# Chunk 6 of an attention and Swish kernel: six pairs of h by half-size products, and the numerators ahead of two groups of h

## The chip, the core and the metric

The kernel runs on one core of one Trainium2 chip. The metric is the device time of one execution in microseconds (us), lower is better. The median of 7 runs of the kernel before is 281.01 us (280.42 to 281.57).

A core has engines that run side by side, each taking its own list of instructions in order: TensorE (PE in the profile; PEld are its weight loads) multiplies matrices into PSUM, an accumulator memory of 8 banks; VectorE (DVE) and ScalarE (ACT) do elementwise work and move results out of PSUM; GpSimd (POOL) and SyncE (SP) mostly issue DMA transfers here. An instruction waits on semaphores for the data and the buffers that it needs, and everything behind it on the same engine's list waits with it.

## The reference

Two stages, one after the other. The first is linear attention with cosine weights over 8 batches, 8 heads, 576 positions and 64 channels:

```
phi(x) = concat(relu(x) * cos(theta), relu(x) * sin(theta))      theta = pi/2 * position / 576
kv  = sum over positions of phi(k)^T v;   z = sum over positions of phi(k)
out = (phi(q) kv) / (phi(q) z + 1e-6)
```

The second takes the result as x, 4608 tokens of 512 features (tokens run over batches and positions), through two matrices with a Swish between them:

```
h = x @ w_in                     # 512 -> 2048
g = h * sigmoid(beta * h)
result = g @ w_out               # 2048 -> 512
```

## The kernel before

**Chunks and batches.** The second stage runs in nine chunks c = 0 to 8 of 512 tokens. For a chunk, h is made in 16 groups of 128 features ("jt" 0 to 15), each 128 features x 512 tokens in one PSUM bank; ScalarE applies Silu with a scale of beta and writes g to SBUF (the factor 1/beta is folded into w_out). Then the output products make the result. While chunk c is worked on, the attention of batch b = c + 1 is done in between: K (the products k^T v on TensorE, L272), kt (kv copied out of PSUM by VectorE, L284), N (the numerators q kv, L293, 144 small matmuls in three parts of 48, each into two neighbouring banks), and x0, x1, x2 (per part: denominators L304, reciprocal L308, multiply L315 on VectorE, and transposing DMAs on SP, L363, that write the next chunks' x). In chunk 6 this is the last batch, b = 7; chunks 7 and 8 have no attention.

**Two ways to make h.** A plain group (`h_plain`, L428; "p0" to "p7" in the order, with its Silu "sp0" to "sp7") is 4 matmuls of 512 columns. A pair of groups can instead be made by `h_fast` (L474): a Winograd form of Strassen's scheme with 7 products instead of 8, each of 2 matmuls of 256 columns, on sums of the weights (made in chunk 4) and on sums t1 to t4 of the chunk's x (VectorE, L873, made for the next chunk during the output products). A pair has three banks (b, e, a) and these operations: products 1, 5, 6, 2, 7, 3, 4 on TensorE; c1 and cu, copies of bank b by ScalarE (L499, L501); c5, a copy of bank e by VectorE (L500); a2, a3, a7, additions by VectorE (L502, L504, L503) that complete the two groups in banks a and b; Sa and Sb, their Silus (L419). So product 3 adds to bank e after c5 has read it, a3 needs product 3 and cu, Sa needs a2 and a3, and Sb needs a7 and product 4. Until Sa and Sb have read the banks, nothing else may write them.

The output products are made in the same way (`o_fast`, L552): two halves x and y of seven products each, of 8 matmuls, on the g of even or odd groups and on sums S1 to S4 of g, which VectorE makes group by group (L399; "s34" is S4 for the last quarter of the groups).

**What sets the order.** Nothing is scheduled by a planner: the order in which the program issues instructions is the order on each engine's list. From chunk 5 on it is written out by hand: `chunk` (L894) walks a string of short names, `ORDER` (L852) for chunks 5 and 6 and `ORDER_END` (L859) for 7 and 8, and issues each name's instructions. "X1" is product 1 of pair X, "c1X" its copy c1, "SaX" its Silu; "ox1" and "oy1" are output products, "c1o" and "c1y" their copies, "o2x" their additions; "s01" is S1 for the first quarter of the groups; "K", "kt", "N0" and "x0" as above; "t1" is a sum of the next chunk's x. Names of one engine keep their order in the string, and names of different engines are tied by data and banks alone.

In `ORDER` four pairs are fast: X (groups 0, 1), Y (4, 5), Z (8, 9), V (12, 13), and eight groups are plain; in `ORDER_END` six are fast, with E (2, 3) and F (6, 7), and four plain. The tables `steady` and `end` in `chunk` give each pair its first group and its banks b, e, a; `plain_bank` gives the plain groups theirs; `parts` (L985) are the first banks of the three parts of N, and `xb`, `yb` (L986) the banks of the output products.

In chunk 6 before, the string's end runs "... V4 s21 s23 s14 SbV s22 N0 sp7 ox1 ...": the numerators come after all 16 groups.

Of the kernel before, what the change touches and what calls it, by code (L numbers as in the profile page):

```python
# [22 lines left out]
def kernel(  # L23
# [16 lines left out]
    B, H, S, D = q.shape  # L40
# [10 lines left out]
    E = D + 1  # L51
# [211 lines left out]
    def kv_out(jp, bank):  # L263
        return ps[:, bank : bank + 2, jp * 2 * E : (jp + 1) * 2 * E]

    def kv_mm(b, jp, bank, jjs=(0, 1)):
        t = kv_out(jp, bank)
        for n in range(NQ):
            for jj in jjs:
                for g in range(2):  # L270
                    hs = slice(g * HP, (g + 1) * HP)
                    nc.tensor.matmul(  # L272
                        t[jj * HP : (jj + 1) * HP, g], lhsT=rk[hs, n, 2 * jp + jj, :],
                        rhs=vb[hs, n, 2 * jp + jj].rearrange("q s e -> q (s e)"),
                        start=(n == 0), stop=(n == NQ - 1))
# [189 lines left out]
    def h_fast(c, jt0, banks):  # L465

        b_bank, e_bank, a_bank = banks
        hf = TCH // 2
        b_ps, e_ps, a_ps = (ps[:, k, 0:hf] for k in banks)
        xt, n = xt_tile(c), NB // 2  # L470

        def prod(dst, left, right, start, stop):
            for g in range(2):
                nc.tensor.matmul(dst, lhsT=left[:, g], rhs=right[:, :, g * HP : (g + 1) * HP], start=start and g == 0,  # L474
                                 stop=stop and g == 1, skip_group_check=True)

        def w(f, jp):
            f += jt0 % 4
            return win[jt0 // 4][:, 2 * jp : 2 * jp + 2, f * P : (f + 1) * P]

        def x(jp, i):
            return xt[:, i * n : (i + 1) * n, jp]

        s1, s2, s3, s4 = (w_sum(jt0, i) for i in range(4))
        t1, t2, t3, t4 = (wx["x"][:, i] for i in range(4))
        p1 = part.tile([P, HM], FP32, name="p1", tag="p1")
        p5 = part.tile([P, HM], FP32, name="p5", tag="p5")
        u = part.tile([P, HM], FP32, name="u", tag="u")

        acc = dict(op=ALU.add)  # L490
        ops = {
            "1": lambda: prod(b_ps, w(0, 0), x(0, 0), True, False),
            "5": lambda: prod(e_ps, s1, t1, True, False),
            "6": lambda: prod(b_ps, s2, t2, False, False),
            "2": lambda: prod(a_ps, w(0, 1), x(1, 0), True, True),
            "7": lambda: prod(b_ps, s3, t3, False, False),
            "3": lambda: prod(e_ps, s4, x(1, 1), False, True),
            "4": lambda: prod(b_ps, w(1, 1), t4, False, True),
            "c1": lambda: nc.scalar.copy(p1, b_ps),  # L499
            "c5": lambda: nc.vector.tensor_copy(p5, e_ps),  # L500
            "cu": lambda: nc.scalar.copy(u, b_ps),  # L501
            "a2": lambda: nc.vector.tensor_tensor(a_ps, a_ps, p1, **acc),  # L502
            "a7": lambda: nc.vector.tensor_tensor(ps[:, b_bank, hf:TCH], b_ps, p5, **acc),  # L503
            "a3": lambda: nc.vector.tensor_tensor(ps[:, a_bank, hf:TCH], e_ps, u, **acc),  # L504
            "Sa": lambda: h_silu(c, jt0, a_bank),
            "Sb": lambda: h_silu(c, jt0 + 1, b_bank),
        }
        return ops
# [336 lines left out]
    def k_piece(b, j):  # L845
# [10 lines left out]
        "sp6 s13 SaV V4 s21 s23 s14 SbV s22 N0 sp7 ox1 s31 ox5 s32 k1 x0 c1o s33 ox6 k0 k2 k3 c5o oy1 "  # L856
        "s24 ox2 s34 g0 g1 v8 w4 v4 x1 c1y o2x ox3 v2 v7 cuo x2 oy6 ox7 oy2 cuy o3x o7x oy5 oy7 ox4 w8 "
        "o2y v6 c5y t1 t3 oy3 w1 w0 o7y t2 v5 v3 oy4 t4 o3y w7 v1 w6 c4x w5 w3 w2 v0 c4y")
    ORDER_END = (  # L859
        "E1 F1 E2 X1 c1E X5 c1X X2 E5 a2E c5X X6 E6 X3 c1F a2X Y1 cuX X7 c5E cuE c1Y E3 E7 Y6 a3X SaX cuY "  # L860
        "a7X a3E Y5 SaE a7E X4 F6 F5 Y7 c5Y E4 Y2 cuF c5F Y3 F7 F2 a7Y a3Y a7F SbX SbE Y4 F3 a2Y Z1 a2F "
# [32 lines left out]
    def chunk(c, b, x, y, parts):  # L894
        steady = {"X": (0, 2, 0, 1), "Y": (4, 3, 4, 5), "Z": (8, 0, 2, 1), "V": (12, 4, 3, 5)}
        end = {"X": (0, 6, 0, 1), "E": (2, 5, 3, 4), "Y": (4, 2, 0, 1), "F": (6, 7, 3, 4), "Z": (8, 6, 0, 1),
               "V": (12, 5, 3, 4)}
        pairs = {n: h_fast(c, at[0], at[1:]) for n, at in (steady if b < B else end).items()}

        def plain_bank(n):  # L900
            return (2 if n == 7 else 6 + n % 2) if b < B else (2, 7)[n % 2]

        plain = [2, 3, 6, 7, 10, 11, 14, 15]
        outs = {"x": x, "y": y}

        def q_next():
            if b + 3 < B:
                load_raw(b + 3, "q")

        def raw_next(name):  # L910
            if b + 2 < B:
                load_raw(b + 2, name)

        xs_all = {"x0", "x1", "x2"}
        take = prep(b, [
            ({"k0", "k1", "k2", "k3"} | xs_all, lambda: raw_next("k")),
            ({"q0", "q1"} | xs_all, q_next),
            ({f"{o}{n}" for o in "vw" for n in range(NQ)}, lambda: raw_next("v"))])
        last_sum = None
        for op in (ORDER if b < B else ORDER_END).split():  # L920
            n = int(op[-1]) if op[-1].isdigit() else None
            if op == "K":
                kv_mm(b, 0, 4)
                kv_mm(b, 1, 4)
            elif op == "kt":
                kv_take((0, 1), 4)
            elif op[0] == "N":
                for t, bank in enumerate(parts):
                    num_all(b, t, bank)
            elif op[0] == "x":  # L930
                x_part(b, n, parts[n])
                take(op)
            elif op[0] in "kvwq":
                take(op)
            elif op[0] == "t":
                if c + 1 < NTC:
                    x_sum(c + 1, n)
            elif op[0] == "g":
                if b + 1 < B:
                    q_tan(b + 1, n, None if n else last_sum)  # L940
            elif op[0] == "p":
                h_plain(c, plain[n], plain_bank(n), 2 if n < SPLITS.get(c, (0, 0))[0] else 1)
            elif op[:2] == "sp":
                h_silu(c, plain[n], plain_bank(n))
            elif op[0] == "o" and n is not None:
                outs[op[1]][op[2]]()
            elif op[0] == "o":
                outs[op[2]]["a" + op[1]]()
            elif op[0] == "c" and op[2] in "xyo":
                outs["x" if op[2] == "o" else op[2]][op[:2]]()  # L950
            elif op[0] == "s":
                last_sum = g_sum(c, 2 * int(op[1]), 2 * int(op[1]) + 2, n)
            else:
                pair = op[0] if op[0] in pairs else op[-1]
                pairs[pair][op.replace(pair, "")]()
        if b + 2 < B:
            q_turn_dma(b + 2)
# [24 lines left out]
    FAST = 5  # L982
    for c in range(2, NTC):
        b = c + 1
        parts = (6, 0, 4) if c < FAST else (0, 6, 4)  # L985
        xb, yb = ((2, 3, 6), (1 if c == FAST - 1 else 7, 3, 6)) if c < FAST else ((3, 2, 0), (1, 2, 0)) if b < B else ((0, 3, 6), (1, 3, 6))  # L986
        x, y = o_fast(c, 0, xb), o_fast(c, 1, yb)
        if c >= FAST:
            chunk(c, b, x, y, parts)
            continue  # L990
        sums = h_first(c)
        for t, bank in enumerate(parts):
            num_all(b, t, bank)
        q_tan(b + 1, 0, sums)
        q_tan(b + 1, 1)
        for i, n in enumerate("156273"):
            x[n]()
            if n in "156":
                x["c" + ("u" if n == "6" else n)]()
                x_part(b, i, parts[i])  # L1000
        for j in range(4):
            k_piece(b + 1, j)
        for n in ("a7", "a2", "a3"):
            x[n]()
        att_q(b + 2, False)
        y["1"]()
        y["c1"]()
        v_half(b + 1, 1, 0, 1, "act")
        x["4"]()
        x["c4"]()  # L1010
        v_half(b + 1, 1, 1, 2, "act")
        v_half(b + 1, 0, 0, 3)
        y["5"]()
        y["c5"]()
        if c == FAST - 1:
            x_sums(c + 1)
        v_half(b + 1, 1, 2, 3, "act")
        y["6"]()
        y["cu"]()
        y["2"]()  # L1020
        y["a2"]()
        v_half(b + 1, 0, 3, 5)
        y["7"]()
        y["a7"]()
        v_half(b + 1, 0, 5, 7)
        y["3"]()
        y["a3"]()
        v_half(b + 1, 0, 7, 9)
        v_half(b + 1, 1, 3, 9, "act")
        y["4"]()  # L1030
        y["c4"]()
        q_turn_dma(b + 2)
# [30 lines left out]
```

## Time and profile before

| | us |
|---|---|
| median of 7 runs | 281.01 |
| profiled execution, its own time | 281.07 |
| its span, first to last instruction | 279.3 |
| TensorE busy | 270.4 (97%) |
| VectorE busy | 210.2 (75%) |
| ScalarE busy | 178.2 (64%) |
| chunk 6, h with K, on the chain | 197.15 to 211.42 |
| chunk 6, numerators | 211.42 to 212.86 |
| chunk 6, output products | 212.86 to 225.19 |
| chunk 7, h | 225.19 to 237.88 |
| granted TensorE clock, mean | 0.998 |

The profile is of one execution. "Busy" counts the time in which an engine worked on an instruction; lengths of single instructions overlap their successors, since engines are pipelined, so the pace of a sequence is read from the starts. In a timeline a row is: start, length, engine, line, operation, out<-in, shapes, count of merged instructions, and in brackets the idle time before it with what ended it. The chain of waits follows back from the last instruction to what released it, step by step.

### The profile page before, as it was taken

The page shows a single profiled execution, that of the slowest core. Times are in us where ns is not written, and L with a number is a line of the kernel's source. Part 1 is how long each engine was busy: PE and PEld are TensorE (multiplying, and loading weights), DVE is VectorE, ACT ScalarE, POOL GpSimd, SP SyncE. Part 2 cuts the span into 40 slices and gives each one's busy share as a digit, 9 for nine tenths or more (in the row PEclk, how much of TensorE's full clock was granted, in tenths as well). Part 3 has the DMA queues.
Part 4 walks back from the last instruction along what each step waited for, and adds up shares of the span by engine and source line. Part 5 has one row for each costly group of instructions (what it writes and reads, how often), then busy time and mean ns, then how long its engine had stood idle before and what let it go on. Part 6 is the DMA issues. An engine that isn't in the chain of part 4 may idle for free.

```text
span 279.3 us, 8732 instructions
## 1 busy us (share of the span) xinstructions
PE 270.4 (97%) x3613; PEld 193.3 (69%) x3619; DVE 210.2 (75%) x539; ACT 178.2 (64%) x348; POOL 70.7 (25%) x89
## 2 busy tenths in 40 slices
PE   8779999999999999999999999999999999999993
PEld 8444455445874588548854798778767886888783
DVE  5789979577999687348749996799679779649832
ACT  5578858774127657675857586896685179529911
POOL 1354000616093063205420452007400140000000
PEclk9999999999999999999999999999999999999999
DMA  7999999999988977991799189906400640033006
GB/s 228 382 389 353 397 388 304 378 207 386 214 254 279 282 207 195 379 211 34 168 364 271 30 182 279 175 10 117 115 2 7 120 113 4 0 76 77 0 2 150
DMA packets 50583, 53.98 MB, mean 193 GB/s; under 512 B 31200, under 2 KB 31472, under 8 KB 50544
## 3 DMA queue, kind: packets, MB, share of 16 engines
q1 hardware_dynamic: 47584, 45.82, 57.3%
q0 software_dynamic: 2688, 7.34, 8.8%
q8 instruction: 28, 0.46, 0.7%
q10 hardware_dynamic: 272, 0.27, 0.4%
q14 instruction: 11, 0.09, 0.2%
HBM read 36.71 MB, written 9.44 MB: 165 GB/s over the span
## 4 chain that ended last, share of the span: by engine, by line
PE 91%; DMA 4%; DVE 2%; issue 1%; SPq 1%; ACTq 0%; ACT 0%
PE ps L552 31%; PE ps L380 25%; PE ps L474 11%; PE ps L523 10%; PE ps L428 7%; PE ps L293 4%; DMA raw_v<-in_v_dram 4%; PE ps L272 3%; SPq L79 1%; DVE xs L315 1%; PE ps L352 0%; DVE win L115 0%; PE ps L234 0%; DVE rden L308 0%; DVE den L304 0%
## 5 line engine op out<-in xcount | busy, mean ns | idle before, releaser
L380 PE MATMUL ps<-xt,win 128*128 128x512 bf16 (+1 forms) x327 | 71.2, 375 | 0.1
L388 ACT ACTIVATE g_t<-ps,beta 128x512 bf16<-128x512 f32 x80 | 54.7, 689 | 19.2 <-PE ps L380 17.9
L380 PEld LDWEIGHTS <-win 128*128 128x128 bf16 x327 | 31.4, 98 | 35.3 <-issue 0.6
L516 POOL DMA_DIRECT2D out_dram<-o_sb x56 | 31.7, 572 | 65.8 <-DVE o_sb L603 33.2
L552 PEld LDWEIGHTS <-S 128*128 128x128 bf16 x476 | 44.3, 98 | 4.8
L419 ACT ACTIVATE g_t<-ps,beta 128x512 bf16<-128x512 f32 x64 | 41.3, 698 | 3.3 <-PE ps L428 2.2
L552 PEld LDWEIGHTS <-g_t 128*128 128x128 bf16 x364 | 33.0, 98 | 3.6
L399 DVE TENSOR_TENSOR S<-g_t 128x512 bf16<-128x512 bf16 (+1 forms) x62 | 22.4, 395 | 11.4 <-ACT g_t L388 9.1
L222 POOL TENSOR_TENSOR qs<-qt,tanr 128x1152 bf16<-128x1152 bf16 x8 | 19.0, 2388 | 47.4 <-DVE S L399 17.2
L523 PE MATMUL ps<-wout,g_t 128*128 128x256 bf16 (+1 forms) x171 | 28.6, 318 | 0.4 <-issue 0.2
L552 PE MATMUL ps<-wout,g_t 128*128 128x256 bf16 (+1 forms) x238 | 28.1, 266 | 0.0
L552 PE MATMUL ps<-wout,S 128*128 128x256 bf16 (+1 forms) x238 | 27.4, 266 | 0.0
L552 PE MATMUL ps<-T,S 128*128 128x256 bf16 (+1 forms) x238 | 27.1, 266 | 0.0
L428 PE MATMUL ps<-xt,win 128*128 128x512 bf16 (+1 forms) x111 | 24.0, 350 | 0.0
L315 DVE TENSOR_TENSOR xs<-ps,rden 128x768 bf16<-128x768 f32 (+4 forms) x26 | 22.8, 884 | 0.8
L523 PEld LDWEIGHTS <-g_t 128*128 128x128 bf16 x177 | 16.9, 98 | 9.2
L217 ACT ACTIVATE vb<-raw_v,sin 128x256 bf16<-128x256 f32 (+1 forms) x50 | 21.9, 501 | 1.2 <-DMA raw_v<-in_v_dram 1.2
L219 DVE TENSOR_SCALAR vb<-raw_v,cos 128x256 bf16<-128x256 f32 x63 | 22.6, 418 | 0.0
L474 PE MATMUL ps<-w_stage 128*128 128x256 bf16 x120 | 20.3, 273 | 0.0
L474 PEld LDWEIGHTS <-w_stage 128*128 128x128 bf16 x160 | 15.5, 98 | 3.9
L222 POOL TENSOR_TENSOR w_stage<-qt,tanr 128x1152 bf16<-128x1152 bf16 x4 | 9.5, 2384 | 27.8 <-DVE den L304 27.8
L428 PEld LDWEIGHTS <-win 128*128 128x128 bf16 x111 | 10.9, 98 | 6.7
(104 smaller groups left out, 384.6 us busy)
## 6 DMA issues: line engine op xcount, KB each, us to landing
raw_v<-in_v_dram SPq DMA_DIRECT2D x7, 1152.0 KB, 10.6
raw_k<-in_k_dram SPq DMA_DIRECT2D x7, 1152.0 KB, 8.6
raw_q<-in_q_dram SPq DMA_DIRECT2D x7, 1152.0 KB, 7.8
out_dram<-o_sb POOLq DMA_DIRECT2D x56, 128.0 KB, 4.9
w_stage<-in_moe_w_in_dram SPq DMA_DIRECT2D x3, 1024.0 KB, 14.1
w_stage<-in_moe_w_out_dram SPq DMA_DIRECT2D x2, 1024.0 KB, 7.7
w_stage<-in_moe_w_out_dram SPq DMA_DIRECT2D x4, 512.0 KB, 11.9
out_dram<-o_sb SPq DMA_DIRECT2D x13, 128.0 KB, 2.4
```

The costliest lines, as they stand in the source:

```text
L219: nc.vector.tensor_scalar(o, a, scalar1=t[:, n : n + 1], scalar2=None, op0=ALU.mult)
L222: return eng.tensor_tensor(dst.rearrange("q n (g p) -> q n g p", g=2), src.rearrange("q n (g p) -> q n g p", g=2), tanr[:, n0:n1].unsqueez ...
L315: nc.vector.tensor_tensor(o.rearrange("q j n s d -> q j (n s) d"), nv[:, :, a:z, :, 0:D].rearrange("q j n s d -> q j (n s) d"), rden[:, :, ...
L380: nc.tensor.matmul(ps[:, h_bank(c, jt), i * 64 : (i + w) * 64], lhsT=win[jt // 4][:, mi, (jt % 4) * P : (jt % 4 + 1) * P], rhs=xt[:, i : i ...
L388: nc.scalar.activation(gs[c, jt // 4][:, jt % 4], ps[:, h_bank(c, jt)], AF.Silu, scale=beta[:, jt : jt + 1])
L399: return nc.vector.tensor_tensor(o, l, r, op=op)
L419: nc.scalar.activation(gs[c, jt // 4][:, jt % 4], ps[:, bank], AF.Silu, scale=beta[:, jt : jt + 1])
L428: nc.tensor.matmul(ps[:, bank, o * 64 : z * 64], lhsT=win[jt // 4][:, mi, (jt % 4) * P : (jt % 4 + 1) * P], rhs=xt[:, o:z, jp, g * HP : (g ...
L474: nc.tensor.matmul(dst, lhsT=left[:, g], rhs=right[:, :, g * HP : (g + 1) * HP], start=start and g == 0, stop=stop and g == 1, skip_group_ ...
L516: eng.dma_start(out=out_v[bb, n][:, m0:m1], in_=o_sb[hf * HP : (hf + 1) * HP, m0:m1])
L523: nc.tensor.matmul(o_ps[:, m0 : m0 + w], lhsT=gs[c, jt // 4][:, jt % 4, tt * P : (tt + 1) * P], rhs=wout[:, jt, m0 : m0 + w], start=(jt == ...
L552: nc.tensor.matmul(dst[:, m : m + w], lhsT=left(i), rhs=right[:, i, m : m + w], start=start and i == 0, stop=stop and i == order[-1], skip ...
```

## The change

Chunk 5 keeps `ORDER`, chunks 7 and 8 keep `ORDER_END`; chunk 6 gets a string of its own, `ORDER_MID`, and tables of its own.

- Groups 2, 3 (pair E) and 6, 7 (pair F) are no longer plain: 16 matmuls of 512 columns become 28 of 256, with two ScalarE copies and four VectorE instructions for each pair.
- K goes to banks 6 and 7 instead of 4 and 5; banks of pairs, plain groups (p4 to p7 in 6, 7, 2, 3) and output products are given anew.
- The numerators N0 stand ahead of the groups p6 and p7: "... SaV s12 s23 SbV s22 s14 N0 p6 sp6 x0 p7 sp7 s31 ox1 ...". Their third part goes to banks 4 and 5, which pair V (banks 5, 3, 4) holds until SaV and SbV.
- All other names are in a new order too; the name "s34" stands in it twice.

The lists of SP and POOL are as before. The lines L873 and above move by 7 or more in the changed file; the lines of the helpers named above do not.

```
--- before.py
+++ after.py
@@ -856,6 +856,13 @@
         "sp6 s13 SaV V4 s21 s23 s14 SbV s22 N0 sp7 ox1 s31 ox5 s32 k1 x0 c1o s33 ox6 k0 k2 k3 c5o oy1 "
         "s24 ox2 s34 g0 g1 v8 w4 v4 x1 c1y o2x ox3 v2 v7 cuo x2 oy6 ox7 oy2 cuy o3x o7x oy5 oy7 ox4 w8 "
         "o2y v6 c5y t1 t3 oy3 w1 w0 o7y t2 v5 v3 oy4 t4 o3y w7 v1 w6 c4x w5 w3 w2 v0 c4y")
+    ORDER_MID = (
+        "E2 E1 X5 c1E X1 c1X c5X X2 a2E E6 E5 X3 X6 cuX c5E a2X a3X K cuE E7 SaX E3 X7 kt a3E Y5 a7X a7E "
+        "Y1 F1 SaE F5 Y2 X4 c1Y c5Y F2 Y3 c1F SbX Y6 E4 c5F cuY a2F a2Y F6 SbE Z1 Y7 F3 cuF c1Z a3Y a7Y "
+        "Z5 V1 SaY c1V F7 c5Z Z6 Y4 Z3 a3F Z2 cuZ V6 a7F s01 SbY F4 SaF cuV a3Z V5 Z7 p4 SbF s02 a7Z V2 "
+        "V7 s03 c5V Z4 a2Z V3 sp4 a2V SbZ a7V SaZ s11 a3V s13 p5 s04 sp5 V4 s21 SaV s12 s23 SbV s22 s14 "
+        "N0 p6 sp6 x0 p7 sp7 s31 ox1 s32 x1 ox5 s24 s34 c1o s34 c5o ox6 oy1 c1y ox2 s33 o2x oy6 x2 ox3 "
+        "cuy cuo oy2 ox7 o3x oy5 o7x ox4 t1 oy7 o2y c5y t2 c4x oy3 t4 t3 o7y oy4 c4y o3y")
     ORDER_END = (
         "E1 F1 E2 X1 c1E X5 c1X X2 E5 a2E c5X X6 E6 X3 c1F a2X Y1 cuX X7 c5E cuE c1Y E3 E7 Y6 a3X SaX cuY "
         "a7X a3E Y5 SaE a7E X4 F6 F5 Y7 c5Y E4 Y2 cuF c5F Y3 F7 F2 a7Y a3Y a7F SbX SbE Y4 F3 a2Y Z1 a2F "
@@ -895,10 +902,15 @@
         steady = {"X": (0, 2, 0, 1), "Y": (4, 3, 4, 5), "Z": (8, 0, 2, 1), "V": (12, 4, 3, 5)}
         end = {"X": (0, 6, 0, 1), "E": (2, 5, 3, 4), "Y": (4, 2, 0, 1), "F": (6, 7, 3, 4), "Z": (8, 6, 0, 1),
                "V": (12, 5, 3, 4)}
-        pairs = {n: h_fast(c, at[0], at[1:]) for n, at in (steady if b < B else end).items()}
+        mid = {"X": (0, 2, 0, 1), "E": (2, 5, 3, 4), "Y": (4, 6, 0, 1), "F": (6, 7, 3, 4), "Z": (8, 2, 0, 1),
+               "V": (12, 5, 3, 4)}
+        pairs = {n: h_fast(c, at[0], at[1:]) for n, at in (steady if c < B - 2 else mid if b < B else end).items()}
+        kv_bank = 4 if c < B - 2 else 6
 
         def plain_bank(n):
-            return (2 if n == 7 else 6 + n % 2) if b < B else (2, 7)[n % 2]
+            if c < B - 2:
+                return 2 if n == 7 else 6 + n % 2
+            return (6, 7, 2, 3)[n - 4] if b < B else (2, 7)[n % 2]
 
         plain = [2, 3, 6, 7, 10, 11, 14, 15]
         outs = {"x": x, "y": y}
@@ -917,13 +929,13 @@
             ({"q0", "q1"} | xs_all, q_next),
             ({f"{o}{n}" for o in "vw" for n in range(NQ)}, lambda: raw_next("v"))])
         last_sum = None
-        for op in (ORDER if b < B else ORDER_END).split():
+        for op in (ORDER if c < B - 2 else ORDER_MID if b < B else ORDER_END).split():
             n = int(op[-1]) if op[-1].isdigit() else None
             if op == "K":
-                kv_mm(b, 0, 4)
-                kv_mm(b, 1, 4)
+                kv_mm(b, 0, kv_bank)
+                kv_mm(b, 1, kv_bank)
             elif op == "kt":
-                kv_take((0, 1), 4)
+                kv_take((0, 1), kv_bank)
             elif op[0] == "N":
                 for t, bank in enumerate(parts):
                     num_all(b, t, bank)
@@ -983,7 +995,7 @@
     for c in range(2, NTC):
         b = c + 1
         parts = (6, 0, 4) if c < FAST else (0, 6, 4)
-        xb, yb = ((2, 3, 6), (1 if c == FAST - 1 else 7, 3, 6)) if c < FAST else ((3, 2, 0), (1, 2, 0)) if b < B else ((0, 3, 6), (1, 3, 6))
+        xb, yb = ((2, 3, 6), (1 if c == FAST - 1 else 7, 3, 6)) if c < FAST else ((3, 2, 0), (1, 2, 0)) if c < B - 2 else ((2, 3, 0), (1, 3, 0)) if b < B else ((0, 3, 6), (1, 3, 6))
         x, y = o_fast(c, 0, xb), o_fast(c, 1, yb)
         if c >= FAST:
             chunk(c, b, x, y, parts)
```

## The prediction

> **What bounds the kernel now.** I read the page's shares first, then the chain of waits in order of time, then the engines' timelines in chunk 6, the only chunk whose instructions change. From the page:
>
> ```profile
> span 279.3 us, 8732 instructions
> ...
> PE 270.4 (97%) x3613; PEld 193.3 (69%) x3619; DVE 210.2 (75%) x539; ACT 178.2 (64%) x348; POOL 70.7 (25%) x89
> ...
> PE 91%; DMA 4%; DVE 2%; issue 1%; SPq 1%; ACTq 0%; ACT 0%
> ```
>
> TensorE is the bound: whatever it is spared, or made to stand, comes off or on the end. The chain by time (start, length, what), chunks 6 and 7:
>
> ```profile
> 197.15 0.66 PE ps L474 x6
> ...
> 199.54 1.15 PE ps L272 x72
> ...
> 211.20 0.22 PE ps L474 x2
> 211.42 1.44 PE ps L293 x129
> 212.86 12.33 PE ps L552 x112
> 225.19 6.78 PE ps L474 x62
> ...
> 237.88 12.23 PE ps L552 x112
> ```
>
> Chunk 6's h begins at 197.15 on this chain, K is the 1.15 at 199.54, the numerators N0 stand at 211.42, the output products start at 212.86. Chunk 7 has six fast pairs already and no attention: its h takes 237.88 - 225.19 = 12.69 us. Nothing but TensorE stands between. Its timeline around the places that the change touches (start, length):
>
> ```profile
> 197.64 1.03 PE L428 MATMUL ps<-xt,win 128*128 128x512 bf16 x4
> 198.50 0.60 PE L474 MATMUL ps<-w_stage 128*128 128x256 bf16 x4
> ...
> 199.16 0.38 PE L474 MATMUL ps<-xt,w_stage 128*128 128x256 bf16 x2
> ...
> 212.14 0.22 PE L293 MATMUL ps<-kv,qs 64*64 64x65 bf16 x4
> 212.27 0.22 PE L293 MATMUL ps<-kv,qt 64*64 64x65 bf16 x4
> ```
>
> Lengths include a tail, so I take differences of starts: four 512-wide matmuls take 0.86 to 0.87, a product of two 256-wide ones 0.218. The hole from 212.14 to 212.27 is N0's third part, which waits for ScalarE's SbV to leave its bank. ScalarE and VectorE (start, length, count):
>
> ```profile
> 210.38 2.42 ACT L419 ACTIVATE g_t<-ps,beta 128x512 bf16<-128x512 f32 x4
> 225.50 0.38 ACT L499 COPY p<-ps 128x256 f32<-128x256 f32 x1
> ...
> 233.79 0.68 ACT L501 COPY u<-ps 128x256 f32<-128x256 f32 x2
> 234.31 4.96 ACT L419 ACTIVATE g_t<-ps,beta 128x512 bf16<-128x512 f32 x8
> ```
> ```profile
> 200.00 0.43 DVE L504 TENSOR_TENSOR ps<-ps,u 128x256 f32<-128x256 f32 x1
> 200.74 0.70 DVE L284 CAST kv<-ps 128x520 bf16<-128x520 f32 x1 [0.31 <-PE ps L272]
> 201.35 0.42 DVE L503 TENSOR_TENSOR ps<-ps,p 128x256 f32<-128x256 f32 x1
> ```
>
> Four Silus in 2.42, the last taking 0.69, are (2.42 - 0.69)/3 = 0.577 apart when nothing holds them; chunk 7's eight are (4.96 - 0.69)/7 = 0.61 apart. A copy costs 0.27 before the next instruction. In the third view kt (the cast) waits for K and all of VectorE's list waits with it.
>
> **The change part by part.**
> *Matmuls.* Four plain groups (16 matmuls of 512) become pairs E and F (28 of 256): 16 x 0.2165 = 3.46 against 28 x 0.109 = 3.05, so 0.41 us less TensorE work. Chunk against chunk agrees: 14.27 (197.15 to 211.42) less K's 1.15 is 13.12, against 12.69. This is on the bounding engine, and all that the change can give, with the 0.13 hole.
>
> *ScalarE and VectorE.* Two more pairs add four copies on ScalarE (c1, cu: 4 x 0.27 = 1.08) and eight 0.34 instructions on VectorE (c5, a2, a7, a3: 2.7); one sum (s34) is listed twice: 0.34 more. By themselves they lie beside TensorE's work. What counts is when ScalarE reaches SbV.
>
> *N0 moved ahead of p6 and p7.* Its third part writes banks 4 and 5, which pair V holds until SaV and SbV. Before, 15 Silus and 8 copies had to be done by then, and after N0 only the output products were left. Now 14 Silus and 12 copies, and 1.73 us of TensorE (p6, p7) still follow. So N0 must come earlier than 212.27 by those 1.73 for nothing to be lost. I walk the new list through.
>
> TensorE starts at 196.99. E2 E1 X5 X1 X2 E6 E5 X3 X6 are nine products: K can begin at 196.99 + 9 x 0.218 = 198.95. Before, the product ahead of K was issued by 199.16 + 0.22 = 199.38, and kt began at 200.74, 1.36 later; so kt begins at 200.31. a3E stands behind kt on VectorE and E3 behind K on TensorE; the instruction behind kt began 0.61 later (200.74 to 201.35), so a3E at 200.92. From an a3 to the Silu of its bank the trace has 0.47 (a3X at 200.00, Silu at 200.47): SaE at 201.39. Up to there ScalarE had five short things to do (two c1, two cu, SaX: 4 x 0.27 + 0.58 = 1.66 us in the 3.8 since c1E); SaE is the head of its list, and c1Y, c1F and all else queue behind it.
>
> From SaE on its list to SbV is 13 Silus and 8 copies: SbV starts at 201.39 + 12 x 0.577 + 8 x 0.267 = 210.45 and ends at 211.14. Before, SbV ended at 210.38 + 2 x 0.577 + 0.69 = 212.22 and the third part went on at 212.27, 0.05 later: now at 211.19. From there to the output products it was 212.79 - 212.27 = 0.52 on the timeline: p6 at 211.71, p7 at 212.58. The first output product (ox1) goes into p6's bank 2 and waits for sp6: p6's end 212.57, 0.20 to the Silu (a plain group issued by 203.45 had its Silu at 203.65), 0.69, 0.05: 213.51. It was 212.79: **0.72 later**. TensorE alone would have reached the third part at 196.99 + 84 x 0.109 + 1.24 (K) + 1.73 (p4, p5) + 0.82 (two parts) = 209.9 to 210.0, so some 1.2 us of standing eat the 0.41.
>
> Both bounds of that 0.72: if ScalarE is never late, ox1 starts at 209.95 + 0.52 + 1.73 + 0.07 = 212.27, 0.52 *earlier*; if its steps are those of chunk 7's run (0.61, and 0.31 for a copy, from the pair of 0.68), 12 x 0.033 + 8 x 0.043 = 0.74 is added, and 0.25 for one more hold like those in front of its Silus: 1.7 later. Mine is a list that always has work, so the free spacing is the nearest row; for a few held links I add 0.1.
>
> A page of the Trainium skill would make it dearer: "ScalarE: Activation LUTs", section "What ACT_TABLE_LOAD costs", gives an ACTIVATE with a pointer operand about 280 ns + 0.833 ns an element, 186 ns with immediates alone, and an overlap of 93 ns back to back. An estimate from it: 614 ns between Silus, 306 between copies, or 0.75 more in my sum, about 282.6. The trace's Silu lasts that page's 0.69 to 0.70, but free ones stand 0.577 apart, so I keep the row.
>
> *After ox1.* sp7 ends at 213.43 + 0.20 + 0.69 = 214.32, ox5 is due at 213.51 + 0.87 = 214.38 in its bank 3. s31 follows sp7 and ends about 214.8; its first reader in ox5 is six matmuls in, 215.03. The x parts come no later against the output products than before; the transposes on SP and the stores on POOL keep their order (neither queue's list changes), and chunk 7's first sums are read a whole output phase later. I cost all this at nothing; its cover is 0.1 to 0.2 us, and the tightest is s31.
>
> *Sum.* The profiled execution took 281.07, 1.77 more than its span, and the median of the runs shown is 281.01, 0.06 below. 281.07 + 0.72 + 0.1 - 0.06 = **281.8 us**, 0.3% slower. About 0.2% (0.56 us) can be told from no change: faster is under 280.45, slower over 281.57.
>
> **The rivals.**
> *ScalarE catches up before N0* (the other side: not slower). In chunk 7 it did 12 copies and 14 Silus from 225.50 to 234.31 + 5 x 0.61 + 0.69 = 238.05, in 12.55 us. From c1E (197.63) that gives 210.18 for SbV, ox1 at about 212.55, 281.07 - 0.24 - 0.06 = 280.8; with no standing at all 280.5. Against it: chunk 7 has no K and no kt between E's products, so its first Silu does not stand. It decides from SaE at 200.67, 0.72 sooner than my walk.
>
> *ScalarE is held again and again.* Pairs share banks closely (E and V on 5, 3, 4; X and Z on 2, 0, 1), so each product may wait for an eviction and each eviction for a product. That is the upper bound: 282.4 to 282.8. For it: chunk 7's 0.61; against it: that list's groups came late from TensorE, these come early.
>
> *VectorE becomes the bound.* It was busy 10.6 of 14.27 us and gets 3.0 more, so it is nearly full. If s31 or a late a3 stands 0.3 longer, 282.1: inside my range, and not told apart by time alone.
>
> **How the numbers follow.** ScalarE late as walked, 0.62, 281.4 to 282.3; caught up, 0.22, 280.5 to 281.4; held, or VectorE, 0.16, up to 282.8. Faster needs nearly the whole 0.52: 0.05. Within 0.2%: most of the caught-up case and the lowest part of mine, 0.21. Slower: 0.74. The range 281.0 to 282.8 leaves out most of the caught-up case; the likeliest case alone is 281.4 to 282.3.
>
> **What would show it.** In the changed profile: L428 has 16 matmuls fewer and L474 28 more; kt starts near 200.3 and SaE near 201.4, behind a3E; from there ScalarE shows no idle time until after SbV near 211.1; the L293 numerators, 1.44 us before, take over 2 us, with holes released by ScalarE's L419; the chain in chunk 6 gets ACT pieces; L552 starts near 213.5; chunks 7 and 8 are only shifted. I am wrong if L293 runs through, if ScalarE idles between SaE and SbV, or if output products or chunk 7 stand where they did not.

## The result, and the profile after

The changed kernel took 281.62 us (median of 21 runs), the kernel before 280.58 (median of all 49 runs made of it; the 7 shown above had 281.01). The ratio is 1.0034, with a 95% interval of 1.0023 to 1.0045: 0.95 us (0.65 to 1.3) slower. Predicted was 281.8 in a range of 281.0 to 282.8, and 0.3% slower.

The page of the changed kernel, the lines that answer to those shown of before:

```profile
span 278.9 us, 8776 instructions
...
PE 270.5 (97%) x3625; PEld 194.1 (70%) x3631; DVE 212.4 (76%) x548; ACT 178.7 (64%) x352; POOL 70.9 (25%) x89
...
PE 89%; DMA 3%; DVE 2%; ACT 2%; SPq 1%; issue 1%; ACTq 0%
```

The span of this one execution is *shorter* than the one shown of before, 278.9 against 279.3. That is no gain: the same instructions up to chunk 6 happened to be 1.25 us sooner (first product of chunk 6 at 195.74, before 196.99). Among the executions profiled in this study that point lies between 195.74 and 199.49. So a stage is compared with a stage: from chunk 6's first product (L474) to its first output product (L552). It took 212.79 - 196.99 = 15.80 us before and takes 212.34 - 195.74 = **16.60** now, 0.80 more. Behind it nothing moved inside the span: chunk 6's output products take 12.23 (before 12.24), chunk 7's h 12.69 in both.

Something moved outside the span. A run's time is always more than its span from first to last instruction: by 1.79 us on average (1.73 to 1.86) in 51 runs of the kernel before, by 2.15 (2.08 to 2.23) in 22 runs of the changed one. So some 0.35 of the 0.95 us lies ahead of the first or behind the last instruction, where no profile shows what it is. The 0.6 that is left for the span can't be told from the stage's 0.80, since runs of one kernel lie up to 2 us apart.

The chain in order of time (start, length, what), in chunk 6, which was TensorE's alone before:

```profile
195.90 1.97 PE ps L474 x18
197.88 1.15 PE ps L272 x72
199.02 5.02 PE ps L474 x44
...
204.89 0.76 ACT g_t L419
...
206.29 3.69 ACT g_t L419 x6
209.98 0.04 issue
210.02 0.57 PE ps L293 x42
210.60 1.83 PE ps L428 x8
212.43 12.30 PE ps L552 x112
```

From 204 to 210 the chain runs through ScalarE's Silus, and p6 and p7 (the 1.83 of L428) come after them. The timelines around it, ScalarE, VectorE and TensorE (start, length, merged count):

```profile
200.15 0.69 ACT L419 ACTIVATE g_t<-ps,beta 128x512 bf16<-128x512 f32 x1 [0.62 <-DVE ps L504]
200.73 0.64 ACT L499 COPY p<-ps 128x256 f32<-128x256 f32 x2
...
205.71 4.26 ACT L419 ACTIVATE g_t<-ps,beta 128x512 bf16<-128x512 f32 x7
211.60 0.69 ACT L419 ACTIVATE g_t<-ps,beta 128x512 bf16<-128x512 f32 x1 [1.63 <-PE ps L428]
```
```profile
199.07 0.70 DVE L284 CAST kv<-ps 128x520 bf16<-128x520 f32 x1 [0.27 <-PE ps L272]
199.69 0.42 DVE L504 TENSOR_TENSOR ps<-ps,u 128x256 f32<-128x256 f32 x1
```
```profile
208.08 0.42 PE L293 MATMUL ps<-kv,qt 64*64 64x65 bf16 x4
...
209.22 0.22 PE L293 MATMUL ps<-kv,qs 64*64 64x65 bf16 x4
209.44 0.22 PE L293 MATMUL ps<-kv,qt 64*64 64x65 bf16 x2
210.02 0.22 PE L293 MATMUL ps<-kv,qt 64*64 64x65 bf16 x2 [0.36 <-ACT g_t L419]
...
210.53 1.90 PE L428 MATMUL ps<-xt,win 128*128 128x512 bf16 x8
```

SaE (200.15) waits for a3E (199.69), which stands behind kt (199.07); the last row but one of TensorE's is N0's third part, going on when SbV ends at 205.71 + 4.26 = 209.97. The numerators take 208.08 to 210.53, 2.45 us where they took 1.44.

### The profile page after: what moved, and what is told of

Same layout as the page of the kernel before. It is cut to its first block, busy times and chain, and to the rows that moved or that the text cites. A ratio compares the mean times of both kernels' runs of the same rounds, so it can differ in the third digit from the quotient of the medians.

```text
span 278.9 us, 8776 instructions
## 1 busy us (share of the span) xinstructions
PE 270.5 (97%) x3625; PEld 194.1 (70%) x3631; DVE 212.4 (76%) x548; ACT 178.7 (64%) x352; POOL 70.9 (25%) x89
## 4 chain that ended last, share of the span: by engine, by line
PE 89%; DMA 3%; DVE 2%; ACT 2%; SPq 1%; issue 1%; ACTq 0%
PE ps L552 31%; PE ps L380 25%; PE ps L474 11%; PE ps L523 10%; PE ps L428 6%; PE ps L293 3%; DMA raw_v<-in_v_dram 3%; PE ps L272 3%; ACT g_t L419 2%; SPq L79 1%; DVE xs L315 1%; PE ps L234 0%; PE ps L352 0%; DVE win L115 0%; DVE vb L209 0%
## 5 line engine op out<-in xcount | busy, mean ns | idle before, releaser
L380 PE MATMUL ps<-xt,win 128*128 128x512 bf16 (+1 forms) x327 | 71.1, 375 | 0.1
L380 PEld LDWEIGHTS <-win 128*128 128x128 bf16 x327 | 31.4, 98 | 35.2 <-issue 0.4
L552 PEld LDWEIGHTS <-S 128*128 128x128 bf16 x476 | 44.3, 98 | 4.8
L552 PEld LDWEIGHTS <-g_t 128*128 128x128 bf16 x364 | 33.1, 98 | 3.9 <-issue 0.2
L552 PE MATMUL ps<-wout,g_t 128*128 128x256 bf16 (+1 forms) x238 | 28.1, 266 | 0.0
L552 PE MATMUL ps<-wout,S 128*128 128x256 bf16 (+1 forms) x238 | 27.3, 266 | 0.0
L552 PE MATMUL ps<-T,S 128*128 128x256 bf16 (+1 forms) x238 | 27.1, 266 | 0.0
L474 PE MATMUL ps<-w_stage 128*128 128x256 bf16 x132 | 22.1, 272 | 0.0
L428 PE MATMUL ps<-xt,win 128*128 128x512 bf16 (+1 forms) x95 | 19.9, 345 | 0.0
L474 PEld LDWEIGHTS <-w_stage 128*128 128x128 bf16 x176 | 17.0, 98 | 3.4
L474 PE MATMUL ps<-xt,win 128*128 128x256 bf16 x88 | 15.3, 273 | 0.0
```

Of the source, the lines that this page charges most:

```text
L380: nc.tensor.matmul(ps[:, h_bank(c, jt), i * 64 : (i + w) * 64], lhsT=win[jt // 4][:, mi, (jt % 4) * P : (jt % 4 + 1) * P], rhs=xt[:, i : i ...
L428: nc.tensor.matmul(ps[:, bank, o * 64 : z * 64], lhsT=win[jt // 4][:, mi, (jt % 4) * P : (jt % 4 + 1) * P], rhs=xt[:, o:z, jp, g * HP : (g ...
L552: nc.tensor.matmul(dst[:, m : m + w], lhsT=left(i), rhs=right[:, i, m : m + w], start=start and i == 0, stop=stop and i == order[-1], skip ...
```

## Experiments

All are edits of the changed kernel, and the measure is the stage above, read from one profiled execution of each. Where an edit is shown shortened, "..." stands for names that stay. Where a name stands twice or three times, the same values are computed again; nothing is left out of any of these kernels.

| kernel | first product to first output product | whole time against before |
|---|---|---|
| before | 15.80 | |
| changed | 16.60 | 1.0034 (1.0023 to 1.0045) |
| N0 behind p6 and p7 | 15.43 | 0.9998 (0.9982 to 1.0014) |
| the same once more | 15.44 | 1.0009 (0.9987 to 1.0031) |
| the same, s34 once | 15.43 | 1.0011 (0.9990 to 1.0033) |
| N0 between p6 and p7 | 15.67 | single run |
| four pairs, N0 moved | 16.93 | 1.0069 (1.0046 to 1.0093) |
| one more Silu | 17.30 | single run |
| two more sums, late | 16.59 | single run |
| two more sums, in the middle | 17.03 | single run |
| two copies from ScalarE to VectorE | 16.79 | single run |
| E3 and a3E ahead of K and kt | 17.04 | single run |

### The two halves of the change, one at a time

N0 behind p6 and p7, six pairs kept:

```diff
-        "N0 p6 sp6 x0 p7 sp7 s31 ox1 s32 x1 ox5 ..."
+        "p6 sp6 p7 N0 sp7 x0 s31 ox1 s32 x1 ox5 ..."
```

> The changed kernel with one thing undone: the numerators N0 stand behind p6 and p7 again (six pairs stay). Measure: from chunk 6's first product (L474) to its first output product (L552); before 15.80 us (196.99 to 212.79), changed 16.60 (195.74 to 212.34). Theory A, the loss comes from the place of N0 (it stands for ScalarE's SaZ, sp5, SaV, SbV while p6 and p7, 1.73 us, are kept back): p6 and p7 cover the wait, the 0.41 us of the matmuls is left, 15.4 to 15.6, the whole 0.1 to 0.4 us under before. Rival B, the four more copies fill ScalarE (1.08 us) wherever N0 stands: 16.2 to 16.6, the whole no faster than before.

Four pairs and the order of before, N0 alone set ahead of p6 and p7 (the sums around it follow; shown against the kernel before):

```diff
-        "sp4 Z7 V3 c1V ... a7V p6 sp5 s12 p7 sp6 s13 SaV V4 s21 s23 s14 SbV s22 N0 sp7 ox1 ..."
+        "sp4 Z7 V3 c1V ... a7V sp5 s12 s13 SaV V4 SbV s14 N0 p6 sp6 s21 s23 p7 sp7 s22 ox1 ..."
...
-            return (2 if n == 7 else 6 + n % 2) if b < B else (2, 7)[n % 2]
+            return ({6: 3, 7: 2}.get(n, 6 + n % 2)) if b < B else (2, 7)[n % 2]
```

> The other half alone: chunk 6 with the four pairs and the order of before, only N0 set ahead of p6 and p7 (these in banks 3 and 2). Theory A: TensorE now reaches V4 and N0 1.73 us sooner than pair V's additions and Silus are done; a7V ended at 210.39 before, then V4 and its Silu 0.22 + 0.20 + 0.69, 0.05, the third part 0.52, p6 and p7 1.73: ox1 at 213.8 where it was 212.79, so 16.8 (16.3 to 17.1), the whole 0.5 to 1.3 us slower. Rival B (the copies are the loss): no copies are added, 15.8, the whole as before.

Measured: 15.43 and 16.93. For the stage theory A holds in both, rival B in neither. The pairs alone give 0.37 of their 0.41 us; the move alone costs 1.13. Together that is 0.76, and the change cost 0.80: the two add up. The new order of all other names and the new banks stay when N0 stands last, so they are not the loss. For the whole time both forecasts missed: 0.1 to 0.4 us under before was expected for the first, and no gain is shown (0.9998); 0.5 to 1.3 over for the second, and it is 1.9 over. With N0 last the chain in chunk 6 is TensorE's alone again:

```profile
199.27 6.31 PE ps L474 x56
205.58 0.86 PE ps L428 x4
206.44 0.87 PE ps L474 x8
207.32 0.86 PE ps L428 x4
208.18 0.22 PE ps L474 x2
208.40 1.73 PE ps L428 x8
210.13 1.36 PE ps L293 x141
211.49 12.33 PE ps L552 x112
```

The 1.73 of p6 and p7 now lie ahead of the numerators, and no Silu stands in the chain. With the move alone TensorE's timeline shows where it stands, and it is not for ScalarE:

```profile
208.79 0.38 PE L474 MATMUL ps<-w_stage 128*128 128x256 bf16 x2
210.13 0.38 PE L474 MATMUL ps<-w_stage,win 128*128 128x256 bf16 x2 [0.95 <-DVE ps L503]
210.44 0.22 PE L293 MATMUL ps<-kv,qt 64*64 64x65 bf16 x4
```

The row at 210.13 is V4, and it waits 0.95 us for a7V on VectorE (L503); by starts it is 1.34 behind the product ahead of it, 1.12 more than a product takes, about as much as the whole loss. After that the numerators run through. So the cover is what counts, and whichever list is behind, ScalarE's or VectorE's, takes the wait. This kernel's output products were also longer, 12.72 us, with sp7 on ScalarE, two sums of g and x0 on VectorE in the chain ahead of 88 of their 112 matmuls; its whole time, 1.9 us over before, holds both, and the expectation had only the first.

### N0 between p6 and p7

```diff
-        "N0 p6 sp6 x0 p7 sp7 s31 ox1 s32 x1 ox5 ..."
+        "p6 N0 sp6 x0 p7 sp7 s31 ox1 s32 x1 ox5 ..."
```

> The changed kernel with N0 between p6 and p7 (in the changed kernel it is ahead of both, in the run with N0 last behind both: 16.60 and 15.43). Theory A, p6 and p7 are cover for the wait: of 1.2 us of standing 0.87 are covered again, the rest stays: 15.65 to 15.8, with N0's third part still held by SbV or sp6. If the place of N0 counts for itself and not the cover (x parts, banks), it lies nearer to one of the ends.

Measured: 15.67. One group of cover (0.87) takes back 0.93 of the 1.17 us, the other only 0.24: the wait is 1.2 us long, and it goes as far as the cover reaches.

### Which list has no slack

One more Silu ahead of N0, and two more sums late on VectorE's list:

```diff
-        "V7 s03 c5V Z4 a2Z V3 sp4 a2V ... SbV s22 s14 "
+        "V7 s03 c5V Z4 a2Z V3 sp4 sp4 a2V ... SbV s22 s14 "
```
```diff
-        "V7 s03 c5V Z4 a2Z V3 sp4 a2V ... SbV s22 s14 "
+        "V7 s03 c5V Z4 a2Z V3 sp4 a2V ... SbV s22 s14 s14 s14 "
```

> The changed kernel with one more Silu on ScalarE's list ahead of N0: sp4 is done twice (the same values again). Theory A says that ScalarE's list has no slack from SaE to SbV: ox1 comes 0.58 later or a little more, 17.2 to 17.35 from the first product. Rival C, VectorE paces the stage: 16.6 to 16.7.

> The changed kernel with two more instructions on VectorE's list ahead of N0's release: the sum s14 is done three times (the same values again), 2 x 0.334 = 0.67 us. Theory A (ScalarE paces): 16.6 (16.55 to 16.7). Rival C, VectorE paces the stage and the x parts behind it: up to 17.3.

Measured: 17.30 (0.70 later) and 16.59 (no later). By these two ScalarE paces the stage and VectorE does not. But the added s14 stand behind all additions of the pairs, and nothing that the numerators or ox1 wait for comes after them, so the second run tests only the end of VectorE's list. The next two spoil the simple reading. The same two sums in the middle of VectorE's list, and two of ScalarE's copies given to VectorE:

```diff
-        "... cuZ V6 a7F s01 SbY F4 SaF cuV a3Z ..."
+        "... cuZ V6 a7F s01 s01 s01 SbY F4 SaF cuV a3Z ..."
```
```diff
+            "du": lambda: nc.vector.tensor_copy(u, b_ps),
...
-        "... Z2 cuZ V6 a7F s01 SbY F4 SaF cuV a3Z ..."
+        "... Z2 duZ V6 a7F s01 SbY F4 SaF duV a3Z ..."
```

> The changed kernel with two more VectorE instructions (0.67 us, the sum s01 done three times, the same values) in the middle of its list, ahead of pair V's and F's additions, where the run with s14 three times had them behind. Stage of the changed kernel 16.60. Theory A2, VectorE's list is nearly full up to V's additions: with 0.2 to 0.3 of slack, 0.35 to 0.5 later, 16.95 to 17.1. Theory A, ScalarE alone: 16.6 to 16.7.

> The changed kernel with two of ScalarE's copies (cu of pairs V and Z) done by VectorE. Stage from chunk 6's first product to its first output product, 16.60 in the changed kernel. Theory A as the prediction had it, ScalarE's list alone sets SbV: 2 x 0.27 us less on it, 16.06 to 16.2. Theory A2, by the stall that fell on VectorE's a7V when N0 alone was moved: VectorE's list is as full as ScalarE's until V's additions, and two more instructions of 0.335 there delay a3V, a7V and V4 by more than ScalarE gains: 16.5 to 16.9.

Measured: 17.03 (0.43 of the 0.67 us arrive) and 16.79, *later* although ScalarE has 0.54 us less to do. In the first the profile names the links: TensorE's V3 stands 0.28 us for c5V (VectorE, L500), and then sp5 on ScalarE stands 0.26 for p5, the plain group behind V3:

```profile
207.80 0.38 PE L474 MATMUL ps<-xt,w_stage 128*128 128x256 bf16 x2 [0.28 <-DVE p L500]
```
```profile
209.08 1.84 ACT L419 ACTIVATE g_t<-ps,beta 128x512 bf16<-128x512 f32 x3 [0.26 <-PE ps L428]
```

In the second, ScalarE's timeline (all of this execution is some 3 us later, see the end):

```profile
207.81 1.89 ACT L419 ACTIVATE g_t<-ps,beta 128x512 bf16<-128x512 f32 x3
210.17 3.73 ACT L419 ACTIVATE g_t<-ps,beta 128x512 bf16<-128x512 f32 x6 [0.47 <-PE ps L428]
```

ScalarE got through its Silus sooner and then stood 0.47 us for p4, a plain group. p4 starts 9.62 after the first product (209.11), in the changed kernel 9.43 (205.17): TensorE has a hole of 0.2 just ahead of it (products at 208.05 and 208.46, 0.22 apart elsewhere), and one of 0.15 at 210.6. TensorE and VectorE (in this run's kernel the lines behind L501 are moved by 2, and L502 is the copy):

```profile
208.05 0.38 PE L474 MATMUL ps<-w_stage 128*128 128x256 bf16 x2
208.46 0.38 PE L474 MATMUL ps<-w_stage,win 128*128 128x256 bf16 x2
```
```profile
207.65 0.41 DVE L502 COPY u<-ps 128x256 f32<-128x256 f32 x1
207.98 0.42 DVE L505 TENSOR_TENSOR ps<-ps,p 128x256 f32<-128x256 f32 x1
```

The profile names no releaser for holes so short, but the times fit: F4 (208.46) needs a7F, which stands behind the copy duZ and ends at 207.98 + 0.42 = 208.40, 0.06 before. The second hole ends in the same way, V3 at 210.78 behind c5V's end at 210.72. The sizes are those of theory A2: up to what pair V's products need, VectorE's list has only 0.2 to 0.3 us of slack, at its end it has more. At these places ScalarE can't be relieved at VectorE's cost.

### SaE sooner

```diff
-        "... a2X a3X K cuE E7 SaX E3 X7 kt a3E Y5 ..."
+        "... a2X a3X cuE E3 a3E K E7 SaX X7 kt Y5 ..."
```

> The changed kernel with E3 and a3E set ahead of K and kt, so that SaE no longer waits for kt. The prediction's rival said that SaE 0.72 us sooner decides: then SbV and ox1 come 0.72 sooner, 15.9 (15.85 to 16.1). Against it (A2): K starts about 0.45 later, since E3 waits for c5E; kt frees banks 6 and 7 that much later, and Y1 and F1, whose copies feed the middle of ScalarE's list, stand for it: 16.8 to 17.1, with SaE sooner and ScalarE idle after it.

Measured: 17.04, 0.44 later. ScalarE at the start of chunk 6, whose first product is at 196.00 here:

```profile
199.11 1.27 ACT L419 ACTIVATE g_t<-ps,beta 128x512 bf16<-128x512 f32 x2 [0.23 <-DVE ps L504]
201.01 0.65 ACT L499 COPY p<-ps 128x256 f32<-128x256 f32 x2 [0.64 <-PE ps L474]
201.84 0.69 ACT L419 ACTIVATE g_t<-ps,beta 128x512 bf16<-128x512 f32 x1 [0.18 <-PE ps L474]
```

The first row merges SaX and SaE: SaE is directly behind SaX, at about 199.69, 3.69 after the first product and not 4.41, so the 0.72 us were won there. They were lost in the next row: c1Y waits 0.64 us for Y1 and starts 5.01 after the first product, where the changed kernel had it at 200.73 - 195.74 = 4.99. The reason is on VectorE and TensorE:

```profile
198.53 1.22 PE L272 MATMUL ps<-vb,rk 64*64 64x130 bf16 x72
...
200.55 0.60 PE L474 MATMUL ps<-xt,win 128*128 128x256 bf16 x4
```
```profile
199.80 0.70 DVE L284 CAST kv<-ps 128x520 bf16<-128x520 f32 x1 [0.39 <-PE ps L272]
```

K (198.53) starts 2.53 after the first product instead of 2.07 (197.81 - 195.74), since E3 stands ahead of it and waits for c5E; kt (199.80) ends at 200.50 and only then are banks 6 and 7 free for Y1 and F1 (200.55). All that follows is later by about that 0.46.

### A version that could beat both

With N0 last the stage is 0.37 us under before in three executions. The listing of s34 a second time costs nothing in it:

```diff
-        "N0 p6 sp6 x0 p7 sp7 s31 ox1 s32 x1 ox5 s24 s34 c1o s34 c5o ..."
+        "p6 sp6 p7 N0 sp7 x0 s31 ox1 s32 x1 ox5 s24 s34 c1o c5o ..."
```

> N0 behind p6 and p7, and the sum s34 listed once: the version that should beat both. Stage 15.4 to 15.5 as with N0 last, against 15.80 before; s34's second turn lay behind the end of h and costs nothing. The whole 0.3 to 0.4 us under before (ratio 0.9987), which five rounds can hardly tell from 1.

> The run with N0 behind p6 and p7 once more, for its whole time: the stage is 0.37 us shorter than before in both profiles of such an order, so the ratio should be 0.9987; the intervals so far, 0.9982 to 1.0014 and 0.9990 to 1.0033, hold 1 as well. If stages outside chunk 6 give the gain back, the ratio stays at 1.000 or above.

The whole times do not show the gain: 0.9998, 1.0011 and 1.0009, all with 1 inside their intervals, and only the first and third reach down to the 0.9987 expected. This order beats the changed kernel. That it beats the one before was not shown; the runs of each kernel spread over 1.2 to 3 us. What takes most of the 0.37 us back can be read from the runs: in the 36 runs of these three the time is 2.13 us more than the span (2.07 to 2.21), against 1.79 in the 51 runs of before, so 0.34 us more lies outside the instructions. The spans alone are 0.18 us shorter on average (278.51 against 278.69), which their scatter does not tell from 0.37. With N0 moved and four pairs the difference is 1.79 in four runs, so it does not come with the move. It is not simply the six pairs either: with two copies given to VectorE it is 1.78, with two more sums 1.89 (single runs). What it consists of is open.

## Why the prediction was right, and where it was not

*The walk.* Its steps, counted from chunk 6's first product, against the changed kernel's timelines:

| step | walked | measured |
|---|---|---|
| kt | 3.32 | 3.33 |
| a3E | 3.93 | 3.95 |
| SaE | 4.40 | 4.41 |
| SbV ends | 14.15 | 14.23 |
| the last third of N0 goes on | 14.20 | 14.28 |
| p6 | 14.72 | 14.79 |
| first output product | 16.52 | 16.60 |

The walk's 0.72 came out as 0.80, and the 0.1 added for held links was the right size. Nearly all of the difference arose between SaE and SbV, 0.07 us: the run of seven Silus took 4.26, (4.26 - 0.69)/6 = 0.595 apart instead of 0.577, which is 0.11 more, and the Silus and copies ahead of it were 0.04 quicker than walked. The Trainium skill's page "ScalarE: Activation LUTs", section "What ACT_TABLE_LOAD costs", whose figures make an estimate of 0.614 for a Silu and 0.75 more for the whole list, was much farther off than the free row, and on the dear side.

*The matmuls.* 0.41 was forecast, 0.37 is what the pairs give alone.

*After ox1.* Costed at nothing, and nothing it was: 12.23 against 12.24.

*The sum.* It carried over 1.77 us between span and time from the kernel before. That term was mis-sized: it is 2.15 in the changed kernel. The forecast of 281.8 came close to 281.62 partly by luck, since a second term was off the other way: the 281.01 of seven runs, from which it started, is 0.43 above the median of all 49 (280.58). The stage, 0.82 forecast and 0.80 measured, is what was right.

*ScalarE and VectorE: "By themselves they lie beside TensorE's work. What counts is when ScalarE reaches SbV."* This step was too narrow. In the changed kernel ScalarE was the one named in the chain, but VectorE's list was nearly as full, with 0.2 to 0.3 us left up to what pair V's products need. With four pairs, without one added copy, the move cost 1.13 us all the same, and VectorE was the one named. The forecast of the stage came out because the list that the walk followed was the one that was last, not because the other had room; VectorE's list behind a3E it did not go through.

*The rival's deciding point, "SaE at 200.67, 0.72 sooner than my walk".* As a sign it was wrong. SaE was brought forward by just that and the stage got 0.44 longer, because the way to it puts K, kt and Y1 0.46 later. Nor would 0.72 have been there to win: a c1 that waits for its product starts 0.46 behind the product's start (in the run above, Y1 at 200.55 and c1Y at 201.01), so with Y1 where the changed kernel has it (199.84), c1Y could have been 0.43 sooner and no more. In the changed kernel SaE came last of several things at the head of ScalarE's list. No run brought it forward with K left in place, so how much of the 0.43 would have reached ox1 is not shown.

*The other rivals.* ScalarE catching up did not happen; held links cost 0.08 and not the 0.74 to 1.0 of the upper end. VectorE as a further bound behind N0 (s31, x0) did not show in the changed kernel; that its list is "nearly full", as that rival says, the runs bear out ahead of N0.

The whole time (0.65 to 1.3 us slower) holds the stage's 0.80, and also the 1.15 of stage and 0.35 outside the span together; it is not precise enough to choose.

## What to carry to other kernels

When a block of matmuls is moved, ask what it was covering: here 1.73 us of two groups stood ahead of the numerators while pair V's banks were being freed, and setting the reuse of these banks ahead of them cost 1.13 us with four pairs and 1.17 with six. A saving of TensorE work (0.4 us) that is paid in copies and additions on two lists that are already full arrived in the stage only when nothing waited for the ends of these lists. Walk the lists in order with the durations of the rows; and before a wait is called the cause, take it away and see what comes next. Compare the whole time with the span too: here 0.35 us came in outside the instructions.

## What the hardware showed that was not expected

In the execution with two copies given to VectorE, TensorE stood 1.97 us in chunk 4's numerators, where the profile names no releaser; this is far ahead of what the edit touches.

```profile
97.38 0.19 PE L293 MATMUL ps<-kv,qt 64*64 64x65 bf16 x1
99.53 0.22 PE L293 MATMUL ps<-kv,qt 64*64 64x65 bf16 x3 [1.97 <-issue]
```

Behind it the granted clock was 0.61 between 99 and 103 us (0.50 from 99.9 to 103.3), where it is 1.00 in the kernel before, and chunk 6 began at 199.49, some 3 us after the others. In the kernel before, the wait named "issue" at about the same place is 0.14 us. The page "TensorE: Matmul & The Clock Gate" of the Trainium skill ("What's actually happening") has the clock halved after an idle window of about 3.4 us; here a stop of 1.97 us went ahead of it. Why TensorE stopped is open. Single executions of this kernel can differ by such an event more than by the whole change.
